# Where the modulation scale is applied: scaled features with one weight copy, against raw features with scaled and raw weight copies

## The chip, the cores and the metric

The kernel runs on one core of a Trainium2 chip. The metric is the device time of one execution in microseconds (us): three runs of the kernel before gave 404.8, 405.15 and 405.16 us, median 405.15. The profile is one further execution of the same program, with every instruction's start and length.

## The reference

The computation is one transformer-like block on x of 2,048 rows and 576 columns, in bfloat16, with six modulation vectors from a small product:

```
mod = silu(c) @ w_mod                      # six vectors of 576: sa, ca, ga, sb, cb, gb
h = layernorm(x) * (1 + ca) + sa
x = x + ga * attention(h, wqkv, w_phi, wo) # linear attention, 32 heads of 18
h = layernorm(x) * (1 + cb) + sb
x = x + gb * (relu(h @ w1) @ w2)           # 576 -> 4608 -> 576
```

In the attention, q and k of each head go through a small matrix w_phi (18 x 18); the features phi are softmax(p) and softmax(-p) side by side. kv is the sum over all rows of phi_k times v, z the sum of phi_k, and each row's output is (phi_q kv) / (phi_q z). All rows of K and V are needed before the first row of Q can be finished.

## The kernel before, in words

The 2,048 rows are 16 tiles of 128. The kernel has two stages. The first, up to about 102.6 us of the profiled execution, loads everything, does the modulation products, the projections K, V and Q of all tiles, kv, and the attention output, output projection and second norm of tiles 0 and 1. The second runs eight times over pairs of tiles: `l1` (first feed-forward product) and `l2` (second one, in a form with seven instead of eight quarter products), with the attention output of the next two tiles hung between. The change touches the first stage alone.

The norm is not applied to x. x is loaded transposed (xT: features on partitions, five chunks of 116), and a projection of a tile is ten matmuls of 288 columns (`proj`, L267): lhsT is xT's chunk, rhs the weight's. Mean and shift come in through four extra rows of the fifth chunk (`rows_copy`, L572, from per-row statistics; and their counterparts in the weights, made by `rows_mm`, `rows_h`, `rows_d`, L261 and L465 to L473, and by `quarters` for Q). The factor 1/std goes into the exponentials (`exps`, L273, ScalarE). w_phi is folded into the K and Q weights on the chip: `fold_all` (L426) for K, `fold_mm` (L250) for Q, products that end in PSUM and are copied to SBUF by ScalarE or VectorE (`f_raw` L437, `raw_copy` L513).

The factor (1 + ca), called `ca1`, is per feature, so it can be put on xT or on the weights. Before, it is put on xT: `x_scale` (L499) multiplies two tiles of xT in place, with five instructions on VectorE or ScalarE, or with one on GpSimd.

The order of the work in the first stage is a written list, `ORDER` (L43). Each word is a job (a function that issues instructions); each engine works through its own instructions in that order and waits on the others by semaphores. The names that matter:

- Z: matmuls on zeros without use (`spin`, L231). sc, sh: modulation products for ca and sa (`mods`, L241, 25 one-column matmuls each). ca: makes `ca1` and, from it, three columns of `m98` (L494); shc: the fourth column.
- FK: the fold of K. fra, frd, frr: copies of the folded K weight. xd, xa, xp: `x_scale` on VectorE, ScalarE, GpSimd.
- bn: row statistics (VectorE); sa, sp: what follows from them (ScalarE, GpSimd); T, Tc: transposed into the four rows.
- KR, VR, QR with Rh, Re, Rd: the weights' four rows. For Q they are four small DMAs (L485).
- K, V, Q: projections of a tile; Ka and Kb are its first four chunks and its last one. eK, eQ: exponentials. sK, rK, pA, pM: sums, reciprocals and scalings of phi_k (VectorE, ScalarE, GpSimd). vE: v out of PSUM, scaled. kv: accumulation, 9 matmuls, in PSUM banks 6 and 7.
- FQ with a chunk's number: the fold of Q, and FQra, FQrd its copies.
- qs, qp, qt: the same sums and scaling for phi_q, and the transposing DMA. sq, qi: phi_q stored to DRAM and read back. wo: output projection weight times ga (GpSimd), which needs ga_row, which comes by gaw and gar (two DMAs through DRAM).
- wl, w2a, w2b: loads of the feed-forward weights into regions R1 and R2 that the first stage's weights held before.
- kz, tp, nu, nO, ot, oc, W, xr, lb, lr, ap, ht, hd, ha: the way of tiles 0 and 1 from kv to the input of `l1`.

A number after a colon is one of four PSUM pairs of banks. A product into a pair waits until the pair's last content has been read. K's folded weight and Q's lie in `wk`, `wq` (region RH), V's is loaded straight to `wv`. SyncE issues the DMAs in the list's order; an issue that has to wait holds those behind it.

Of the kernel before, what the change touches and what calls it, by code (L numbers as in the profile page):

```python
# [7 lines left out]
P = 128  # L8
# [4 lines left out]
ACT = mybir.ActivationFunctionType  # L13
# [5 lines left out]
NC = 5  # L19
# [21 lines left out]


ORDER = """  # L43
Z11 sx sd rp sc bn1 Z2 bn0 FK ca sa0 sp0 fra0 frd4 sh fra1 frr fra2 xd0 T0:0 fra3 Z2 shc Tc0 Ka0:2 bn2 bn3
KR:1 xd2 sa2 Ka1:0 KRh0 sp2 KRh1 KRd0 Z2 KRd1 T2:1 Kb0 Tc2 Kb1 eKa0 FQ4:1 Z2 FQrd4 eKa1 bn4 FQ3:2 VR:1 sK0
FQra3 xp6 FQ1:0 VRh0 K2:2 FQra1 sK1 rK0 K3:0 VRh1 VRd0 rK1 VRd1 pA0 eK2 bn5 pM0 V0:1 eK3 sK2 m2:2 pA1 sa4 pM1
vE0 V1:0 m2c rK2 sK3 xa4 kv0 pA2 V3:2 sp4 vE1 pM2 bn7 kv1 rK3 T4:1 V2:0 bn9 Tc4 pA3 xa8 vE3 pM3 K4:1 vE2 K5:2
bn6 xp10 eK4 bn8 ga:0 kv2 eK5 sK4 kv3 V4:1 sa6 sK5 sa8 V5:2 sp6 gac sp8 rK4 bn12 rK5 T6:0 pA4 Tc6 wl0 pA5 vE4
xa12 K6:0 pM4 vE5 bn14 FQ0:1 K7:2 pM5 FQrd0 eK6 bn15 kv4 wl3 gb:1 eK7 xp14 kv5 sK6 V7:0 gbc sK7 rK6 T8:2 V6:1
Tc8 pA6 bn11 w2a1 rK7 K8:2 pM6 vE6 bn10 eK8 K9:1 pA7 w2a0 vE7 pM7 sa10 kv6 sK8 V8:2 eK9 sp10 bn13 kv7 rK8 gbw  # L50
T10:0 V9:1 wl1 Tc10 pA8 sK9 sa12 pM8 sa14 K10:0 vE8 rK9 K11:2 pA9 eK10 sp12 vE9 gbr pM9 wl4 kv8 eK11 V10:1
sK10 sp14 T12:0 sK11 w2a2 V11:2 rK10 Tc12 pA10 pM10 vE10 K13:0 rK11 w2b0 K12:1 eK13 pA11 vE11 pM11 kv9 eK12
T14:0 sK13 V13:2 Tc14 sK12 FQ2:1 rK13 K14:0 wl2 pA13 pM13 FQrd2 rK12 kv10 eK14 vE13 kv11 QR:1 K15:2 pA12 QRh
sK14 pM12 V14:0 gaw eK15 QRe QRd V15:1 rK14 sK15 pA14 gar V12:2 pM14 vE14 rK15 Q0:0 vE12 pA15 wo1 vE15 kv12
eQ0 Q1:2 pM15 Q2:1 qs0 eQ1 wo4 kv13 eQ2 kv14 qs1 kv15 qp0 Q3:0 sq2 tp0 Q4:2 qp1 eQ3 qt0 tp2 Q5:1 eQ4 sq3 wo3
tp1 qt1 Q6:0 eQ5 kz wo0 sq4 Q7:2 eQ6 wo2 qi2 nu0:3 Q8:1 w2b1 nO0 eQ7 nu1:0 eQ8 ot0:3 nO1 Q9:2 oc0 ot1:1 Q10:0
eQ9 sq6 sq7 W0:3 oc1 eQ10 sq9 W1:2 xr0 sq5 lb0 Q11:1 sq10 xr1 sq8 lr0 Q12:0 lb1 eQ11 Q13:3 ap0 qi3 lr1 eQ12
sq11 ht0:2 ap1 Q14:1 hd0 ha0 sq12 ht1:0 ha1 hd1 Q15:2 eQ14 qi4 eQ15 sq14 eQ13 sq15 sq13
"""

@with_exitstack
def tile_block(ctx, tc, a, out):
# [132 lines left out]
    def flat(v):  # L195
        return v.rearrange("p a b -> p (a b)")
# [2 lines left out]
    load(act, ident[:], "ident")  # L199
    load(sp, ccol[:], "cc")  # L200
    load(sp, flat(wsc), "wsc")
    load_x(0, 2)
    load(sp, flat(wkT), "wkT")
    load(sp, flat(wsh), "wsh")
    load_xT(0)
# [5 lines left out]
    load_x(4, 2)  # L211
    load_xT(2)
    load(sp, flat(wcb), "wcb")
    load(sp, flat(wsb), "wsb")
# [23 lines left out]
            dve.bn_stats(out=s[:, hf, :], in_=x_sb[:, t, hf * HD:(hf + 1) * HD])  # L238
        dve.bn_aggr(out=mv[:, n, t, :], in_=s)

    def mods(w, width, bank):  # L241

        o = PS[:, bank, :] if isinstance(bank, int) else bank[:, 0, :]
        for k, wm in enumerate(w):
            for ci in range(NC):
                for ck in range(NC):
                    pe.matmul(o[0:width, k * NC + ci:k * NC + ci + 1], lhsT=wm[0:R, ck, ci * width:(ci + 1) * width],  # L247
                              rhs=siluc[0:R, ck:ck + 1], start=(ck == 0), stop=(ck == NC - 1))
# [9 lines left out]
    def v2(ap):  # L258
        return ap.rearrange("p (b f) -> p b f", b=2)
# [174 lines left out]

    last = PS[0:R, 5, 0:NC * FW].rearrange("p (c f) -> p c f", f=FW)

    def f_raw(eng, ck):  # L437
        if eng is act:
            act.activation(out=wk[0:R, ck, 0:G5], in_=PS[0:R, ck, 0:G5], func=ACT.Copy)
        else:  # L440
            eng.tensor_copy(out=wk[0:R, ck, 0:G5], in_=PS[0:R, ck, 0:G5])

    w1a = carve(R1, 0, (4, DFF))
    w1b = R1[:, 4 * DFF:]
# [20 lines left out]
    def rows_h(pr, k):  # L465
        c = slice(k * HD, (k + 1) * HD)
        act.activation(out=tmpr[X0:NX, c], in_=pr[X0:NX, k, 0:HD], func=ACT.Copy)

    def rows_d(pr, dst, k):

        c = slice(k * HD, (k + 1) * HD)
        dve.scalar_tensor_tensor(out=dst[X0:NX, 4, c], in0=tmpr[X0:NX, c], scalar=mk[X0:NX, :],
                                 in1=pr[X0:NX, k, 0:HD], op0=ALU.mult, op1=ALU.add)  # L473

    def part(i):
        return ytb[:, D + i * QW:D + (i + 1) * QW]
# [19 lines left out]
        dve.tensor_scalar(out=m98[0:R, :, X0:X0 + 3], in0=ca1[0:R, :].unsqueeze(2).to_broadcast([R, NC, 3]), scalar1=-1.0,  # L496
                          scalar2=None, op0=ALU.mult)

    def x_scale(t, eng):  # L499

        xT, o, nt, j = XOFF[t]
        if eng is pool:
            v = xT[0:R, o:o + NC * nt * P].rearrange("p (c f) -> p c f", c=NC)[:, :, j * P:(j + 2) * P]
            pool.tensor_tensor(out=v, in0=v, in1=ca1[0:R, :].unsqueeze(2).to_broadcast([R, NC, 2 * P]), op=ALU.mult)
            return
        for ck in range(NC):
            v, f = xt(t, ck, 2), ca1[0:R, ck:ck + 1]
            if eng is act:
                act.activation(out=v, in_=v, func=ACT.Copy, scale=f)
            else:  # L510
                dve.tensor_scalar(out=v, in0=v, scalar1=f, scalar2=None, op0=ALU.mult)
# [77 lines left out]
    def k_minus(t):  # L589
# [376 lines left out]
```

The softmax here doesn't subtract the row's maximum and nothing guards it: scores larger than these inputs give would overflow.

## Time and profile before

| | us |
|---|---|
| median of three runs | 405.15 |
| the profiled execution's own time | 405.16 |
| its span, first to last instruction | 403.4 |
| TensorE busy in the span | 387.7 (96%) |
| VectorE, ScalarE, GpSimd busy | 238.0, 157.0, 147.3 |
| TensorE, VectorE, ScalarE, GpSimd busy in the first 100 us | 92.0, 70.3, 67.2, 55.5 |
| first matmul of `l1` (end of the first stage) | 102.57 |

The profile gives, for each engine, busy time and instructions; a row of tenths in 40 slices of the span; the chain of work that ended last; groups of instructions by line; and for any stretch the list of instructions in order of time. "PEclk" is the share of TensorE's full clock that was granted, in tenths. A product of ten matmuls of 288 columns goes by in 1.23 us at the full clock, one of nine for kv in 0.35 us.

### The profile page before, as it was taken

The numbers are of one execution on the slowest core, as the hardware profiler recorded it, in microseconds if no ns is written. First come the engines' busy times: TensorE is split into PE (matmuls) and PEld (weight loads), VectorE is DVE, ScalarE is ACT, GpSimd is POOL, SyncE is SP. The second block draws the span as 40 slices with busy tenths as digits, with TensorE's granted clock in tenths as the row PEclk, the third lists the DMA queues.
The fourth block names the chain that finished last, engine by engine and source line by source line (L and its number), as shares of the span: only waits on it lengthen the run. The fifth ranks groups of instructions, "written<-read, shape, count | busy, mean of one in ns | idle before, by whom it ended". The sixth has DMA issues, their size and how long they took to land.

```text
span 403.4 us, 8950 instructions
## 1 busy us (share of the span) xinstructions
PE 387.7 (96%) x3701; PEld 313.5 (78%) x3702; DVE 238.0 (59%) x463; ACT 157.0 (39%) x376; POOL 147.3 (37%) x202
## 2 busy tenths in 40 slices
PE   7999999878999998999999999999999999999996
PEld 4877788766887887778877887788788778878885
DVE  2689987845679955664655564547545646514222
ACT  2399887676741143103510530243034104402410
POOL 2157976760200341460066008301810470062045
PEclk9599999999999999999999999999999999999999
DMA  8999495187641155153006410610170061010000
GB/s 298 421 419 384 154 369 185 46 227 271 193 106 34 31 87 126 29 55 85 19 16 89 93 34 10 154 34 17 32 122 18 16 89 34 18 16 32 2 0 32
DMA packets 49517, 44.36 MB, mean 110 GB/s; under 512 B 39362, under 2 KB 42051, under 8 KB 48707
## 3 DMA queue, kind: packets, MB, share of 16 engines
q1 hardware_dynamic: 49186, 43.59, 38.6%
q8 instruction: 29, 0.48, 0.5%
q10 hardware_dynamic: 288, 0.19, 0.2%
q14 instruction: 14, 0.11, 0.1%
HBM read 27.97 MB, written 6.49 MB: 85 GB/s over the span
## 4 chain that ended last, share of the span: by engine, by line
PE 78%; DMA 7%; POOL 4%; DVE 4%; ACT 2%; issue 2%; SPq 1%; POOLq 0%; DVEq 0%; ACTq 0%
PE PS L671 31%; PE PS L731 23%; PE PS L270 9%; PE PS L678 5%; DVE h L857 3%; PE PS L804 3%; ACT RT L275 2%; DMA R<-in_wkT_dram 2%; PE PS L387 1%; DMA eqd<-RT 1%; PE PS L404 1%; POOL RH L743 1%; POOL RT L287 1%; DMA h<-xn 1%; PE PS L247 1%
## 5 line engine op out<-in xcount | busy, mean ns | idle before, releaser
L671 PE MATMUL PS<-h,R 128*128 128x256 bf16 x1152 | 134.3, 273 | 2.1 <-DVE h L857 2.1
L671 PEld LDWEIGHTS <-R 128*128 128x128 bf16 x1152 | 111.1, 98 | 18.8 <-issue 5.9
L731 PEld LDWEIGHTS <-RH 128*128 128x128 f16 x846 | 82.8, 98 | 20.8
L717 POOL TENSOR_TENSOR yt<-yt,gb_row 128x288 f32<-128x288 f32 x23 | 16.8, 729 | 187.3 <-DVE yt L716 187.3
L685 ACT ACTIVATE RH<-PS 128x256 f16<-128x256 f32 x72 | 27.5, 382 | 116.0 <-PE PS L678 101.0
L731 PE MATMUL PS<-R,RH 128*128 128x288 bf16 (+1 forms) x558 | 72.4, 286 | 0.0
L687 DVE SCALAR_TENSOR_TENSOR RH<-PS,RH 128x256 f16<-128x256 f32 x72 | 28.8, 413 | 62.7 <-ACT RH L685 62.7
L275 ACT ACTIVATE RT<-PS,rs 128x576 bf16<-128x576 f32 x64 | 42.7, 750 | 12.6 <-PE PS L270 7.0
L686 ACT ACTIVATE RH<-PS 128x512 f16<-128x512 f32 x72 | 42.9, 596 | 6.2 <-PE PS L671 5.2
L731 PE MATMUL PS<-RT,RH 128*128 128x288 f16 x288 | 37.9, 286 | 0.0
L735 ACT ACTIVATE RS<-PS 128x288 f32<-128x288 f32 x24 | 9.8, 410 | 69.2 <-PE PS L731 69.2
L270 PE MATMUL PS<-RH,RT 116*128 116x288 bf16 x240 | 31.8, 286 | 2.1 <-ACT RT L275 2.0
L270 PE MATMUL PS<-RH,R 116*128 116x288 bf16 x240 | 32.9, 291 | 0.5 <-ACT R L573 0.5
L743 POOL TENSOR_TENSOR RH<-RH,RT 128x2304 f16<-128x2304 f16 x7 | 31.8, 4548 | 0.0
L270 PEld LDWEIGHTS <-RT 116*128 116x128 bf16 x240 | 23.0, 98 | 8.1 <-issue 2.5
L270 PEld LDWEIGHTS <-R 116*128 116x128 bf16 x240 | 23.2, 99 | 7.0 <-issue 0.9
L238 DVE BATCH_NORM_STATS2 st<-x_sb 128x6 f32<-128x288 bf16 x64 | 25.9, 447 | 3.8 <-DMA x_sb<-in_xk_dram 3.2
L716 DVE TENSOR_TENSOR yt<-PS,RS 128x288 f32<-128x288 f32 x23 | 10.4, 451 | 29.7 <-POOL RH L743 24.0
L718 POOL TENSOR_TENSOR x_sb<-yt,x_sb 128x288 bf16<-128x288 f32 x31 | 22.4, 730 | 2.4 <-DVE yt L714 0.6
L280 DVE TENSOR_REDUCE Rk<-RT 128x64 f32<-128x1152 bf16 x16 | 21.1, 1343 | 2.3 <-ACT RT L275 2.0
L280 DVE TENSOR_REDUCE Rq<-RT 128x64 f32<-128x1152 bf16 x16 | 21.3, 1328 | 1.2 <-ACT RT L275 1.2
L409 DVE TENSOR_TENSOR x_sb<-x_sb,PS 128x576 bf16<-128x576 bf16 x16 | 12.0, 751 | 15.5 <-PE PS L804 8.1
(119 smaller groups left out, 439.3 us busy)
## 6 DMA issues: line engine op xcount, KB each, us to landing
R<-in_w1a_dram SPq DMA_DIRECT2D x4, 1152.0 KB, 14.3
eqd<-RT SPq DMA_DIRECT2D x14, 288.0 KB, 5.0
RT<-eqd SPq DMA_DIRECT2D x14, 288.0 KB, 3.0
R<-in_w2a_dram SPq DMA_DIRECT2D x3, 864.0 KB, 8.1
R<-in_w2b_dram SPq DMA_DIRECT2D x2, 1296.0 KB, 9.5
out_dram<-x_sb SPq DMA_DIRECT2D x15, 144.0 KB, 2.2
RT<-in_xT_dram SPq DMA_DIRECT2D x2, 640.0 KB
x_sb<-in_xk_dram SPq DMA_DIRECT2D x3, 288.0 KB
```

The lines of the kernel that those rows point to most:

```text
L238: dve.bn_stats(out=s[:, hf, :], in_=x_sb[:, t, hf * HD:(hf + 1) * HD])
L270: pe.matmul(pr[:, k, 0:HD], lhsT=xt(t, ck), rhs=w[0:R, ck, k * HD:(k + 1) * HD], start=(ck == 0), stop=(ck == NC - 1))
L275: act.activation(out=E.rearrange("p (b h s e) -> p b h s e", b=2, s=2, e=DH)[:, :, :, s, :], in_=pr[:, :, 0:HD].rearrange("p b (h e) -> p ...
L280: dve.tensor_reduce(out=Rr, in_=E.rearrange("p (c e) -> p c e", e=DH), axis=AXX, op=ALU.add)
L671: pe.matmul(PS[:, 2 * u + hf, n * 256:n * 256 + 256], lhsT=w1a[:, ci, jj * P:(jj + 1) * P], rhs=hb[:, ci, :], start=(n == 0 and ci == 0), ...
L678: pe.matmul(PS[:, 2 * u + hf, n * 256:n * 256 + 256], lhsT=w1b[b0:b0 + 64, j * P:(j + 1) * P], rhs=hb[b0:b0 + 64, 4, :], start=False, stop ...
L685: act.activation(out=A11[:, j, :], in_=lo[:, :, 0, :], func=ACT.Relu)
L686: act.activation(out=A2[:, j, :, :], in_=PS[:, 2 * u + 1, :].rearrange("p (n s f) -> p n s f", n=2, s=2), func=ACT.Relu)
L687: dve.scalar_tensor_tensor(out=U3[:, j, :], in0=lo[:, :, 1, :], scalar=0.0, in1=A11[:, j, :], op0=ALU.max, op1=ALU.subtract)
L718: pool.tensor_tensor(out=x_sb[:, t, c], in0=y, in1=x_sb[:, t, c], op=ALU.add)
L731: pe.matmul(PS[:, bank, 0:HD], lhsT=am[:, j, :], rhs=bm[:, j, :], start=first and j == 0, stop=(j % 9 == 8), skip_group_check=True)
L743: pool.tensor_tensor(out=A12, in0=A12, in1=U2, op=ALU.subtract)
```

## The change

`x_scale` is gone, and xT stays as it is loaded. The folded weights of K and Q are copied out of PSUM twice: once scaled by `ca1` into `wk` and `wq` (new jobs fs and fsd for K, fsr for its last 72 columns, FQs for Q) and once as they are into a new region `wfold` (fra, frd, frr, FQra, FQrd), which only the row products read. V's weight is loaded raw to a new region `wv_raw`, and five VectorE instructions (wsd) write it scaled to `wv`. The K and V row copies are one instruction over 576 columns where they were two over 288. `mods` gets a matmul on zeros ahead of each of its five groups in sc and sh (`idle=6`); of the separate Z matmuls 14 are left of 19. The first loads come in another order. And the list `ORDER` is a new one throughout the first stage, so that nearly every job changes its place: Q0 stands after K13 where it stood after V15, and qs0, qp0 and qt0 come forward with it; gbr, gaw and gar stand behind qt0; the five wo stand behind qp1; sq5 stands ahead of w2b1, and sq6 behind sq8. The second stage is the same.

```diff
+    wv_raw = carve(R1, 12760, (NC, D))
+    wfold = carve(R1, 15640, (NC, D))
...
-    load_x(0, 2)
     load(sp, flat(wkT), "wkT")
-    load(sp, flat(wsh), "wsh")
     load_xT(0)
+    load(sp, flat(wsh), "wsh")
+    load_x(0, 2)
+    load(sp, flat(wv_raw), "wv")
     load_x(2, 2)
     load_xT(1)
-    load(sp, flat(wv), "wv")
+    load_x(4, 2)
...
-    def mods(w, width, bank):
+    def mods(w, outs, width, bank, idle=None):
...
             for ci in range(NC):
+                if idle is not None:
+                    spin(1, idle)
...
+    def f_scaled_d(dst, ck):
+        dve.tensor_scalar(out=dst[0:R, ck, 0:G5], in0=PS[0:R, ck, 0:G5], scalar1=ca1[0:R, ck:ck + 1], scalar2=None, op0=ALU.mult)
+    def f_scaled(dst, ck):
+        act.activation(out=dst[0:R, ck, 0:G5], in_=PS[0:R, ck, 0:G5], func=ACT.Copy, scale=ca1[0:R, ck:ck + 1])
     def f_raw(eng, ck):
-            act.activation(out=wk[0:R, ck, 0:G5], in_=PS[0:R, ck, 0:G5], func=ACT.Copy)
+            act.activation(out=wfold[0:R, ck, 0:G5], in_=PS[0:R, ck, 0:G5], func=ACT.Copy)
...
-    def x_scale(t, eng):
...
+    def wv_scale(ck, eng):
+        o, i, f = wv[0:R, ck, :], wv_raw[0:R, ck, :], ca1[0:R, ck:ck + 1]
...
-    ROWS = {"K": wk, "V": wv, "Q": wq}
+    ROWS = {"K": wfold, "V": wv_raw, "Q": wfold}
+    ROWD = {"K": wk, "V": wv, "Q": wq}
...
+        "FQs": lambda c: act.activation(out=v2(wq[0:R, c, :]), in_=at["FQ", c][0:R, :, 0:HD], func=ACT.Copy, scale=ca1[0:R, c:c + 1]),
```

The head and the tail of the new list:

```
Z11 sx sd rp sc FK ca Z2 fs0 fsr frr fra2 sh frd4 fra0 fra1 bn1 fs3 bn0 fs1 Z1 fra3 shc sa0 wsd2 KR:0 fsd4 fs2
sp0 bn2 T0:2 VR:1 KRh bn3 Tc0 Ka0:2 KRd sa2 wsd1 sp2 VRh Kb0 wsd0 Ka1:0 wsd4 eKa0 VRd Kb1 wsd3 T2:1 eKa1 sK0
V0:2 Tc2 sK1 FQ3:0 rK0 K3:1 FQra3 pA0 FQs3 pM0 vE0 eK3 K2:0 bn4 bn5 rK1 kv0 eK2 FQ1:2 pA1 V1:1 sK3 pM1 FQra1
...
tp2 Q5:2 eQ4 sq3 tp1 wo3 nu0:3 eQ5 Q6:0 sq4 nO0 wo0 qi2 Q7:1 eQ6 wo1 sq5 ot0:2 w2b1 eQ7 nu1:3 Q8:0 nO1 oc0
Q9:1 eQ8 W0:3 eQ9 sq7 xr0 lb0 ot1:2 sq8 Q10:0 oc1 sq6 lr0 W1:1 ap0 eQ10 sq9 xr1 lb1 ht0:2 sq10 Q11:0 ha0 hd0
lr1 Q12:3 eQ11 ap1 Q13:2 qi3 eQ12 sq11 ht1:0 Q14:1 hd1 ha1 sq12 eQ13 Q15:3 qi4 eQ14 sq13 eQ15 sq14 sq15
```

More of the change, by code (lines that the diff above doesn't have):

```diff
@@ L43 @@
 ORDER = """
[L44 to L58, printed above, removed]
+Z11 sx sd rp sc FK ca Z2 fs0 fsr frr fra2 sh frd4 fra0 fra1 bn1 fs3 bn0 fs1 Z1 fra3 shc sa0 wsd2 KR:0 fsd4 fs2
@@ new lines @@
+sp0 bn2 T0:2 VR:1 KRh bn3 Tc0 Ka0:2 KRd sa2 wsd1 sp2 VRh Kb0 wsd0 Ka1:0 wsd4 eKa0 VRd Kb1 wsd3 T2:1 eKa1 sK0
+V0:2 Tc2 sK1 FQ3:0 rK0 K3:1 FQra3 pA0 FQs3 pM0 vE0 eK3 K2:0 bn4 bn5 rK1 kv0 eK2 FQ1:2 pA1 V1:1 sK3 pM1 FQra1
+m2:0 vE1 rK3 sa4 pA3 sK2 FQs1 kv1 sp4 V2:1 m2c pM3 bn7 rK2 T4:2 V3:0 bn6 Tc4 pA2 vE2 pM2 sa6 K4:2 vE3 K5:1
+bn10 eK4 sp6 bn9 T6:0 kv2 Tc6 kv3 eK5 sK4 ga:2 K7:0 gac sK5 rK4 K6:1 eK7 pA4 pM4 bn8 V4:2 eK6 sK7 gb:0 sa8
+V5:1 vE4 wl0 rK7 sp8 rK5 sK6 pA7 T8:2 gbc kv4 pA5 Tc8 FQ2:0 pM5 K8:2 vE5 rK6 FQrd2 K9:1 bn11 eK8 w2a2 pA6 pM6
@@ new lines @@
+bn14 kv5 sa10 V6:2 FQs2 sK8 eK9 sp10 wl1 V7:0 pM7 vE6 rK8 sK9 T10:1 V8:2 Tc10 pA8 vE7 pM8 K10:1 rK9 vE8 w2a0
+kv6 bn12 eK10 FQ0:0 pA9 FQ4:2 kv7 pM9 FQrd0 kv8 FQrd4 V9:1 FQs0 w2b0 bn13 FQs4 QR:0 vE9 K11:2 QRh sa12 QRe
+sK10 sp12 kv9 eK11 V10:1 bn15 QRd wl4 rK10 T12:0 V11:2 sK11 Tc12 pA10 sa14 pM10 K13:0 gbw vE10 rK11 wl2 Q0:1
+pA11 eK13 sp14 vE11 pM11 kv10 eQ0 T14:2 sK13 K12:0 w2a1 Tc14 qs0 kv11 rK13 K14:1 eK12 pA13 pM13 V13:2 eK14
+sK12 wl3 K15:0 qp0 vE13 rK12 sK14 V12:1 eK15 pA12 pM12 qt0 Q1:2 vE12 rK14 sK15 gbr V14:0 pA14 eQ1 gaw pM14
@@ L59 @@
+kv12 vE14 rK15 kv13 V15:1 qs1 pA15 gar pM15 kv14 Q2:2 vE15 qp1 kv15 eQ2 Q3:0 tp0 wo4 qt1 kz Q4:1 eQ3 wo2 sq2
+tp2 Q5:2 eQ4 sq3 tp1 wo3 nu0:3 eQ5 Q6:0 sq4 nO0 wo0 qi2 Q7:1 eQ6 wo1 sq5 ot0:2 w2b1 eQ7 nu1:3 Q8:0 nO1 oc0
+Q9:1 eQ8 W0:3 eQ9 sq7 xr0 lb0 ot1:2 sq8 Q10:0 oc1 sq6 lr0 W1:1 ap0 eQ10 sq9 xr1 lb1 ht0:2 sq10 Q11:0 ha0 hd0
+lr1 Q12:3 eQ11 ap1 Q13:2 qi3 eQ12 sq11 ht1:0 Q14:1 hd1 ha1 sq12 eQ13 Q15:3 qi4 eQ14 sq13 eQ15 sq14 sq15
 """
@@ L201, in tile_block @@
     load(sp, flat(wsc), "wsc")
+    load(sp, flat(wkT), "wkT")
+    load_xT(0)
+    load(sp, flat(wsh), "wsh")
     load_x(0, 2)
-    load(sp, flat(wkT), "wkT")
-    load(sp, flat(wsh), "wsh")
-    load_xT(0)
+    load(sp, flat(wv_raw), "wv")
     load_x(2, 2)
     load_xT(1)
-    load(sp, flat(wv), "wv")
+    load_x(4, 2)
     load(sp, epsr[:], "epsr")
     load(sp, flat(wqT), "wqT")
-    load_x(4, 2)
     load_xT(2)
@@ L435, in tile_block @@
     last = PS[0:R, 5, 0:NC * FW].rearrange("p (c f) -> p c f", f=FW)
+    def f_scaled_d(dst, ck):
+        dve.tensor_scalar(out=dst[0:R, ck, 0:G5], in0=PS[0:R, ck, 0:G5], scalar1=ca1[0:R, ck:ck + 1], scalar2=None, op0=ALU.mult)
+    def f_scaled(dst, ck):
+        act.activation(out=dst[0:R, ck, 0:G5], in_=PS[0:R, ck, 0:G5], func=ACT.Copy, scale=ca1[0:R, ck:ck + 1])
     def f_raw(eng, ck):
         if eng is act:
-            act.activation(out=wk[0:R, ck, 0:G5], in_=PS[0:R, ck, 0:G5], func=ACT.Copy)
+            act.activation(out=wfold[0:R, ck, 0:G5], in_=PS[0:R, ck, 0:G5], func=ACT.Copy)
         else:
-            eng.tensor_copy(out=wk[0:R, ck, 0:G5], in_=PS[0:R, ck, 0:G5])
+            eng.tensor_copy(out=wfold[0:R, ck, 0:G5], in_=PS[0:R, ck, 0:G5])
     w1a = carve(R1, 0, (4, DFF))
@@ L463, in t_part, with rows_h, rows_d @@
         eng.tensor_tensor(out=o[:, j, :], in0=p[:, j, :], in1=q[:, j, :], op=ALU.subtract)
[L465 to L473, printed above, removed]
+    def rows_h(pr):
+        act.activation(out=v2(tmpr[X0:NX, :]), in_=pr[X0:NX, :, 0:HD], func=ACT.Copy)
+    def rows_d(pr, dst):
+        dve.scalar_tensor_tensor(out=v2(dst[X0:NX, 4, :]), in0=v2(tmpr[X0:NX, :]), scalar=mk[X0:NX, :],
+                                 in1=pr[X0:NX, :, 0:HD], op0=ALU.mult, op1=ALU.add)
     def part(i):
@@ L497, in scale @@
                           scalar2=None, op0=ALU.mult)
-    def x_scale(t, eng):
[L501 to L511, printed above, removed]
     def raw_copy(eng, o, i):
@@ L517, in raw_copy @@
             eng.tensor_copy(out=o, in_=i)
+    def wv_scale(ck, eng):
+        o, i, f = wv[0:R, ck, :], wv_raw[0:R, ck, :], ca1[0:R, ck:ck + 1]
+        if eng is act:
+            act.activation(out=o, in_=i, func=ACT.Copy, scale=f)
+        else:
+            eng.tensor_scalar(out=o, in0=i, scalar1=f, scalar2=None, op0=ALU.mult)
     def turn(src, pr):
@@ L603, in tile_block @@
         "sd": silu, "ca": scale,
-        "sc": lambda: mods([wsc], R, 7),
-        "sh": lambda: mods([wsh], R, 7),
+        "sc": lambda: mods([wsc], None, R, 7, idle=6),
+        "sh": lambda: mods([wsh], None, R, 7, idle=6),
         "shc": lambda: dve.tensor_copy(m98[0:R, :, X0 + 3], PS[0:R, 7, 0:NC]),
         "FK": lambda: fold_all(wkT),
+        "fs": lambda c: f_scaled(wk, c), "fsd": lambda c: f_scaled_d(wk, c),
         "frd": lambda c: f_raw(dve, c), "fra": lambda c: f_raw(act, c),
-        "frr": lambda: dve.tensor_copy(out=wk[0:R, :, G5:D], in_=last),
+        "fsr": lambda: dve.tensor_tensor(out=wk[0:R, :, G5:D], in0=last,
+                                         in1=ca1[0:R, :].unsqueeze(2).to_broadcast([R, NC, FW]), op=ALU.mult),
+        "frr": lambda: dve.tensor_copy(out=wfold[0:R, :, G5:D], in_=last),
         "rp": lambda: pool.tensor_copy(rep[0:R], siluc[0:R, :].unsqueeze(2).to_broadcast([R, NC, 32])),
-        "xd": lambda t: x_scale(t, dve), "xp": lambda t: x_scale(t, pool), "xa": lambda t: x_scale(t, act),
+        "wsd": lambda c: wv_scale(c, dve), "wsa": lambda c: wv_scale(c, act), "wsp": lambda c: wv_scale(c, pool),
         "bn": lambda t: bn(0, t), "sa": stats_a, "sp": stats_p,
@@ L619, in tile_block @@
         "FQ": lambda c: fold_chunk(c, at["FQ", c]),
-        "FQrd": lambda c: raw_copy(dve, v2(wq[0:R, c, :]), at["FQ", c][0:R, :, 0:HD]),
-        "FQra": lambda c: raw_copy(act, v2(wq[0:R, c, :]), at["FQ", c][0:R, :, 0:HD]),
+        "FQs": lambda c: act.activation(out=v2(wq[0:R, c, :]), in_=at["FQ", c][0:R, :, 0:HD], func=ACT.Copy, scale=ca1[0:R, c:c + 1]),
+        "FQrd": lambda c: raw_copy(dve, v2(wfold[0:R, c, :]), at["FQ", c][0:R, :, 0:HD]),
+        "FQra": lambda c: raw_copy(act, v2(wfold[0:R, c, :]), at["FQ", c][0:R, :, 0:HD]),
         "Q": lambda t: proj(at["Q", t], t, wq), "eQ": lambda t: exps(t, at["Q", t], EQ[:, SLOT[t], :]),
         "sq": q_out, "qi": q_in, "qs": q_sm, "qp": q_pool, "qt": q_turn,
-        "m2": lambda: mods([wsb, wcb], P, at["m2", None]), "m2c": lambda: mod2_e(at["m2", None]),
+        "m2": lambda: mods([wsb, wcb], None, P, at["m2", None]), "m2c": lambda: mod2_e(at["m2", None]),
         "wo": lambda c: pool.tensor_tensor(out=wo_sb[:, c, :], in0=wo_sb[:, c, :], in1=ga_row[:], op=ALU.mult),
@@ L638, in tile_block @@
         JOBS[w + "R"] = lambda w=w: rows_mm(ROWS[w], at[w + "R", None])
-        for k in range(2):
-            JOBS[f"{w}Rh{k}"] = lambda w=w, k=k: rows_h(at[w + "R", None], k)
-            JOBS[f"{w}Rd{k}"] = lambda w=w, k=k: rows_d(at[w + "R", None], ROWS[w], k)
+        JOBS[w + "Rh"] = lambda w=w: rows_h(at[w + "R", None])
+        JOBS[w + "Rd"] = lambda w=w: rows_d(at[w + "R", None], ROWD[w])
     for i, w in enumerate("Q"):
@@ L645, in tile_block @@
         JOBS[w + "Re"] = lambda w=w, i=i: quarter_d(at[w + "R", None], i)
-        JOBS[w + "Rd"] = lambda w=w, i=i: quarter_rows(i, ROWS[w])
+        JOBS[w + "Rd"] = lambda w=w, i=i: quarter_rows(i, ROWD[w])
     for w, m, g in (("ga", wga, 0), ("gb", wgb, 1)):
```

## The prediction

> **What bounds the kernel now.** I read the page first. Its first line puts TensorE at 96% of the span; the row of tenths shows one hole in its clock, in the second slice (10.1 to 20.2 us):
>
> ```profile
> PE 387.7 (96%) x3701; PEld 313.5 (78%) x3702; DVE 238.0 (59%) x463; ACT 157.0 (39%) x376; POOL 147.3 (37%) x202
> PEclk9599999999999999999999999999999999999999
> ```
>
> Then the first stage in windows, with edges where the clock changes: it falls at 8.50 and is back at 18.75. That is 10.25 us, three times 3.41. Columns are length, then busy time of PE, weight loads, VectorE, ScalarE, GpSimd, then the granted clock.
>
> ```profile
> 5.09:8.50 3.41, 2.56 (x30) 1.55 (x28) 1.67 (x5) 0.00 (x0) 0.19 (x1) 1.00 1.03 417
> 8.50:11.92 3.42, 3.30 (x32) 3.31 (x33) 0.98 (x5) 2.55 (x7) 0.65 (x3) 0.50 1.03 413
> 11.92:15.33 3.41, 3.19 (x26) 2.66 (x27) 2.97 (x13) 0.38 (x1) 0.00 (x0) 0.50 1.00 416
> 15.33:18.75 3.42, 3.42 (x16) 2.63 (x15) 1.59 (x9) 1.00 (x4) 0.81 (x3) 0.50 1.04 421
> ```
>
> Next the timeline of TensorE in that stretch (start, length, what, what it waited for):
>
> ```profile
> 6.07 1.49 PE L247 MATMUL PS<-siluc,R 116*116 116x1 bf16 x25 [0.37 <-DMA R<-in_wsc_dram]
> 7.42 0.59 PE L233 MATMUL PS<-zero 128*128 128x512 bf16 x2
> 8.62 2.80 PE L432 MATMUL PS<-RS,R 126*116 126x126 bf16 x25 [0.60 <-DMA R<-in_wkT_dram]
> 11.22 2.64 PE L247 MATMUL PS<-siluc,R 116*116 116x1 bf16 x25
> 16.72 2.38 PE L264 MATMUL PS<-RH,RS 116*100 116x288 bf16 x10
> ```
>
> K's row product (L264) takes 2.38 us here and, later at full clock, V's takes 1.40. From 24 to 71 us TensorE runs on almost without a gap. Last, the timeline from there to the end of the stage, for its idle brackets:
>
> ```profile
> 77.09 0.52 PE L320 MATMUL PS<-RT 128*128 128x76 bf16 x9 [1.16 <-POOL RT L287]
> 84.69 0.55 PE L387 MATMUL PS<-kvz,RE 128*128 128x76 bf16 x10 [0.95 <-DMA RE<-RT]
> 88.44 1.39 PE L270 MATMUL PS<-RH,RT 116*128 116x288 bf16 x10 [0.66 <-ACT RT L275]
> 99.11 1.39 PE L270 MATMUL PS<-RH,RT 116*128 116x288 bf16 x10 [1.33 <-ACT RT L275]
> ```
>
> So the stage is bound by TensorE at half clock, then by TensorE at full clock with VectorE nearly full beside it (9.80 of 10 us in both slices from 30 to 50), then by waits: GpSimd behind ga_row (wo1 waited 2.36 us for it at 74.14, and pM15, qp0, qp1 stood behind it), the transposing DMA behind those, and at 97.68 ScalarE's eQ11, 2.56 us behind the store sq5. What follows 102.57 is the same code in both kernels and starts from l1's first matmul: a shift of that start is carried to the end.
>
> [...] The window that lost the clock streamed columns for some 1.03 us (0.60 of the first Z, 0.43 of the two at 7.42), 30%; the windows 83.60 to 87.02 and 97.26 to 100.67, with 47% and about 44% by the same count, kept it. [...] For VectorE's wsd, 116x576 from SBUF, L418's 414 ns for the same shape is the nearest row[...].
>
> **The change, start of the stage.** Laid out by hand: each engine's jobs in the new order, each as soon as its inputs and its engine are ready, with the trace's durations (back to back where they overlap).
> - Loads move at 0.43 MB/us. wsc lands at 6.07 as before; wkT now follows it, 0.74 MB, so 7.8 (before 8.5). xT0 8.6, wsh 10.3, x tiles 0-1 at 11.0 (before 6.8), wv 12.7, x 2-3 13.4.
> - sc: 25 matmuls at 0.06 and five Z at 0.213: 5.9 to 8.45. In the window to 8.50 the columns streamed are then 0.60 + 5 x 0.213 = 1.67 us, 49%, above the 44% that kept the clock: I take it that the clock stays full. FK from 8.45, 25 matmuls at 0.06 (L255's pace at full clock): 10.0. Z2 10.4, sh 2.5 us: 12.9. The next two windows come to about 65% and 57%.
> - ScalarE: fs0 9.05, then six more at 0.51 to 0.58: fra3 ends 12.8. The doubled copies cost 2.1 us on ScalarE (fs) and 1.2 on VectorE (fsr, fsd4), all ahead of the first product. VectorE from 10.2: fsr 0.5, frr 0.5, frd4 0.65, bn1 and bn0 1.96, shc: 14.0.
> - KR waits for shc, and T0, VR and Ka0 are queued behind it; fs2 is behind sa0, which waits for bn0. KR 14.0 to 15.3, T0, VR to 16.75, Ka0 to 17.7, Kb0 (after KRd, 17.8) 18.1. The first exponential starts at 18.3 where it started at 21.07.
> - Then sK0, V0 (after VRd and wsd3) to 21.1, and with a wait of 0.7 for FQs3 on the way, V1 ends at 26.85. By then K0 to K3, V0, V1, KR, VR, two FQ and kv0 are done. Before had K0 to K3, V0, KR, VR and three FQ by 28.2: after is 1.35 us earlier and V1 (1.23) and kv0 (0.8) less one FQ (0.31) further. **3.1 us ahead.**
>
> **The middle.** Removed: 10 instructions of L511 (2.1 us back to back) from VectorE, 15 of L509 (6.3) from ScalarE, 3 of L504 (2.32 each, 7.0) from GpSimd. Added there: wsd 5 x 0.33 = 1.7 on VectorE, FQs 5 x 0.65 = 3.2 on ScalarE. Merging K's and V's row copies saves some 0.3 us on each. Since TensorE and VectorE set the pace here, GpSimd's 7 us are worth nothing by themselves. From 26.85 TensorE has 28 products of K, V and Q (34.3), three FQ (0.95), kv1 to kv13 (4.7), six T (0.8), m2 1.27, ga and gb 0.86, QR 0.43: 43.3, to 70.15. VectorE, laid out beside it, is full but for 1.5 us in all and holds TensorE up by 0.5. V15 ends at 70.7, with Q0, Q1, kv12 and kv13 done too; before, the last V product ended at 71.05 without them. That is 0.35 + 2 x 1.23 + 2 x 0.35 = **3.5 us ahead**, 0.4 more than at the start. On SyncE: QRd is issued from 53.6 and lands at 58.2, Q0 needs it at 59.0; FQ0 waits for wl1's transfer (its region overlaps the Q weight), issued at 41.3, 1.18 MB, landed by 46, needed at 49.6; qt0 stands ahead of gbr, gaw, gar and holds them until qp0 ends at 66.1, so ga_row lands at about 73.5, and wo4 is due at 74.5. All three are covered, by 0.8, 3.6 and 1.0 us; lost cover costs the excess, on TensorE.
>
> **The tail.** From 70.7: 14 Q (17.2), kv14 and 15 (0.7), nu 0.74, ot and ht 1.1, W 2.46: 22.2 us of products. Before, from 71.05: 25.3 of products, and 102.57 was reached, so 6.2 us of waits (4.9 of them in brackets). pM15 and qp1 no longer stand behind wo; qt0 and qt1 are done before nu needs them; sq5 is issued ahead of the 1.3 MB of w2b1. In the layout pM15 ends at 72.25, qp1 at 74.5, the five wo (1.27 each) at 80.9, nO0 at 80.6, W0 runs at 83.9 and W1 at 86.6, ht1 at 92.6. The waits come to 2.5 us (kv15 for pM15, ot0 for nO0 behind tp1 and tp2, ht1 for eQ11): l1 at 95.4, 7.2 us earlier. But a layout by hand has no late semaphores or queueing DMAs, so I allow the tail twice that, 5.0: l1 at 97.9, **4.7 us earlier**. Against the profiled execution's own 405.16 (median 405.15, the same): 400.5.
>
> Bounds of what the trace doesn't show: the clock kept (0) or lost for one window at 15.33 (1.7 us of the 3.41) or from 8.50 on (below); tail waits from 2.5 to 6.2.
>
> **The rivals.**
> - Slower: the clock falls at 8.50 all the same[...]. Then FK takes 2.80 (to 11.25), Z2 0.85, sh 2.44 + 5 x 0.43 = 4.6 (to 16.7), KR 2.38, T0, VR 2.38 (to 22.0); [...] eKa0 at 23.5, 5.2 us later than laid out. With the tail's waits as before (6.2, not 5.0): 400.5 + 5.2 + 1.2 = 406.9. It decides once more than 4.7 us go. For it: FK at 70 to 80% of the window 8.50 to 11.92 didn't raise the clock before. Against: the 44% that kept it.
> - No change: the stage is VectorE's. To the last vE it has 61 us of work from 10.2 on; in the layout it idles 1.5 us; before, it idled some 5 us between 55 and 75. If it does so again 3.5 us of the gain go, and 404.1 is left; with a late ga_row beside it, 405.
> - A partial gain: the clock lost only at 15.33, KR being late by 1 us: 402.2 to 403.
>
> **How the numbers follow.** The gain as worked out, 398.0 (the layout's 7.2) to 402.0: 0.48. Partial, to 404.3: 0.12. Within 0.2% of 405.15, 404.3 to 406.0, which is about what a measurement of this kernel can tell from no change: 0.10. Slower, by the clock, 406 to 408: 0.30. The likeliest gives 400.5, with its own range 398.0 to 402.0. The range over the cases is 398.0 to 407.0: 0.05 lie below, 0.12 above.
>
> **What would show it.** Right: a granted clock of 1.00 from 5 to 20 us, eKa0 at 18.3, V15's end near 71 with Q0 and Q1 done, no wait of GpSimd for ga_row, l1's first matmul at 96 to 99. Wrong: PEclk of 5 in the second slice, and FK at 2.8 us; VectorE with brackets of 0.5 us and more from 30 to 60; TensorE waiting for FQs copies (a pair of banks now freed by two copies instead of one); or a second stage that waits for weights loaded later.

## The result, and the profile after

The changed kernel takes 396.14 us (median of four runs, 395.76 to 396.28) against 404.98 (404.75 to 405.16): a ratio of 0.9781, 95% interval 0.9764 to 0.9798. It was forecast faster, at 400.5, and the range ended at 398.0: the way was right and the size was not, 8.8 us where 4.7 were expected. Measured again later, the changed kernel came out at 395.94 and 395.76, while single executions of the kernel before spread from 400.45 to 406.54. The stretch at half clock that its profile shows, its clock hole of 10.25 us, is of changing length from one execution to the next (6.82 us in a profile below), so a comparison with it has to say which hole it means.

The page of the changed kernel, the same two lines:

```profile
PE 383.6 (97%) x3706; PEld 310.7 (79%) x3707; DVE 237.8 (60%) x458; ACT 156.6 (40%) x368; POOL 139.3 (35%) x199
PEclk9999999999999999999999999999999999999999
```

The 5 in the second slice of the clock is gone. GpSimd has lost 8.0 us of busy time, 7.0 of them the three products of `x_scale`; ScalarE and VectorE have lost next to nothing, as new copies took the place of the old products. The windows (length, busy time of PE, weight loads, VectorE, ScalarE, GpSimd, granted clock, share and rate of DMA) at the same edges:

```profile
5.09:8.50 3.41, 3.41 (x31) 2.29 (x29) 0.00 (x0) 0.00 (x0) 0.19 (x1) 1.00 1.01 405
8.50:11.92 3.42, 3.36 (x51) 2.92 (x51) 1.99 (x6) 2.81 (x6) 0.00 (x0) 1.00 1.00 410
11.92:15.33 3.41, 2.66 (x28) 2.21 (x28) 3.34 (x11) 2.09 (x6) 0.65 (x3) 1.00 1.06 420
15.33:18.75 3.42, 3.42 (x31) 2.93 (x30) 3.18 (x10) 2.70 (x7) 0.61 (x3) 1.00 1.01 419
```

TensorE's timeline from the fold on, and then the end of the stage (start, length, what, in brackets the idle time ahead and what ended it):

```profile
8.65 1.58 PE L436 MATMUL PS<-RS,R 126*116 126x126 bf16 x25
13.92 1.40 PE L268 MATMUL PS<-R,RS 116*100 116x288 bf16 x10 [0.75 <-DVE RS L608]
...
82.38 1.26 PE L408 MATMUL PS<-wo_sb,oT 128*128 128x288 bf16 x9 [0.31 <-POOL wo_sb L631]
86.61 0.45 PE L529 MATMUL PS<-ident,xn 128*128 128x128 bf16 x5 [0.24 <-DVE xn L422]
87.41 3.83 PE L274 MATMUL PS<-RH,RT 116*128 116x288 bf16 x30 [0.34 <-ACT RT L279]
93.81 3.22 PE L676 MATMUL PS<-h,R 128*128 128x256 bf16 x28
```

The fold runs in 1.58 us instead of 2.80, K's row product (L268) in 1.40 instead of 2.38. At the end three brackets of 0.2 to 0.35 us stand where before there were six of 0.29 to 1.33, and the first matmul of `l1` is at 93.81, 8.76 us earlier than at 102.57. From there to the end of the span it is 300.6 us, against 300.8 before: the whole gain was made in the first stage.

### The profile page after: what moved, and what is told of

It reads as the page before. It is cut to its first block, busy times and chain, and to the rows that moved or that the text cites. A ratio compares the mean times of both kernels' runs of the same rounds, so it can differ in the third digit from the quotient of the medians.

```text
span 394.4 us, 8939 instructions
## 1 busy us (share of the span) xinstructions
PE 383.6 (97%) x3706; PEld 310.7 (79%) x3707; DVE 237.8 (60%) x458; ACT 156.6 (40%) x368; POOL 139.3 (35%) x199
## 4 chain that ended last, share of the span: by engine, by line
PE 79%; DVE 6%; POOL 5%; DMA 4%; ACT 3%; issue 2%; SPq 0%; POOLq 0%; DVEq 0%; ACTq 0%
PE PS L676 32%; PE PS L736 24%; PE PS L274 8%; PE PS L683 5%; DVE h L862 3%; PE PS L809 3%; POOL wo_sb L631 2%; PE PS L408 2%; PE PS L235 2%; ACT RT L279 1%; PE PS L391 1%; POOL RH L748 1%; DMA gatd<-gt 1%; DMA h<-xn 1%; DVE st L240 1%
## 5 line engine op out<-in xcount | busy, mean ns | idle before, releaser
L274 PE MATMUL PS<-RH,R 116*128 116x288 bf16 x240 | 31.8, 286 | 0.5 <-ACT RH L625 0.5
```

The lines of the kernel that those rows point to most:

```text
L274: pe.matmul(pr[:, k, 0:HD], lhsT=xt(t, ck), rhs=w[0:R, ck, k * HD:(k + 1) * HD], start=(ck == 0), stop=(ck == NC - 1))
```

## The experiments

All times are medians. "The tail" is the first stage from the last V product on. Theory C says that the gain came from the clock and from the order of the tail, theory S that it came from the place of the scale, that is from the work taken off the engines by dropping `x_scale`.

### The spins alone

```diff
+    def mods(w, width, bank, idle=None):
...
+                if idle is not None:
+                    spin(1, idle)
...
+        "sc": lambda: mods([wsc], R, 7, idle=6),
+        "sh": lambda: mods([wsh], R, 7, idle=6),
```

> The kernel before with one thing added: a matmul on zeros ahead of each of the five groups in the two modulation products sc and sh (ten in all). Theory C (clock and order): the window 5.09 to 8.50 then streams about 49% instead of 30%, the clock stays at 1.00 from 5 to 20 us, the fold FK takes 1.5 us instead of 2.8, the first exponential starts near 18 instead of 21.07, and the time falls by about 3 us, to 401.5 to 402.5. Rival S (place of the scale): the gain of the change came from the work that x_scale took off GpSimd, ScalarE and VectorE; the spins alone give under 1 us, 404 to 405. If the clock falls all the same, the ten spins cost 1 to 2 us: 406.

Measured: 400.91 against 403.39, ratio 0.9942 (0.9921 to 0.9964), about 2.3 us, a little faster than expected. What these 2.3 us are is told by the mean granted clock that was taken with each execution. The 10.25 us at half clock of the profile before, in 403.4, make a mean of 0.987. The later executions of the kernel before, 39 in all, and those with the spins, by this clock; in brackets, as an estimate, the time at half clock that it stands for, twice the share that is missing of some 403 us:

| mean granted clock | kernel before: executions, us | with the spins: executions, us |
|---|---|---|
| 0.985 to 0.987 (10 to 12 us) | 13, 403.94 to 405.74, median 404.81 | none |
| 0.989 to 0.992 (6 to 9 us) | 10, 403.05 to 403.97, median 403.43 | none |
| 0.996 (3 us) | none | 2, 401.80 and 402.81 |
| 0.998 to 1.00 (under 2 us) | 11, 400.45 to 401.71, median 401.07 | 18, 399.28 to 401.46 |

Five more of the kernel before have 0.998 to 1.00 and took 404.51 to 406.54; no trace explains these. For the others the spins are worth what a kept clock is worth: about 4 us against an execution with 10 to 12 us at half clock, next to nothing against one with under 2. The 2.3 us lie between because the kernel before had both kinds.

The profiled execution is the slowest of the 20, 402.81 us, so its end is not the usual one. The clock stays at 1.00 over its whole start (5.09 to 18.75) and the fold takes 1.56 us; the products K2, K3, V0 begin at 20.53 instead of 24.36, 3.8 us earlier. But in this execution `l1` starts only 1.4 us earlier, at 101.17. ScalarE's timeline and TensorE's show where the rest went; the first line is the same place in the kernel before, the second the kernel with the spins:

```profile
97.68 1.38 ACT L275 ACTIVATE RT<-PS,rs 128x576 bf16<-128x576 f32 x2 [2.56 <-DMA eqd<-RT]
95.17 1.38 ACT L277 ACTIVATE RT<-PS,rs 128x576 bf16<-128x576 f32 x2 [3.47 <-DMA eqd<-RT]
```

```profile
73.66 0.52 PE L322 MATMUL PS<-RT 128*128 128x76 bf16 x9 [1.54 <-POOL RT L289]
96.60 1.39 PE L272 MATMUL PS<-RH,RT 116*128 116x288 bf16 x10 [2.24 <-ACT RT L277]
```

eQ11 waits for the store sq5 3.47 us (2.56 before), TensorE behind it 2.24 (1.33 before), and pM15 1.54 (1.16 before). The last microsecond is in the clock, window by window (granted clock third from the end):

```profile
98.00:99.00 1.00, 0.72 (x6) 0.64 (x6) 0.39 (x2) 1.00 (x4) 0.00 (x0) 0.54 0.68 262
99.00:100.00 1.00, 1.00 (x6) 0.62 (x5) 0.92 (x4) 1.00 (x3) 0.00 (x0) 0.50 0.81 308
100.00:101.00 1.00, 1.00 (x6) 0.63 (x5) 1.00 (x1) 0.98 (x2) 0.00 (x0) 0.50 0.47 71
101.00:102.00 1.00, 1.00 (x9) 0.78 (x8) 0.54 (x2) 0.59 (x1) 0.27 (x2) 0.75 0.76 279
```

The longer wait left ten matmuls in the 3.4 us before 98.1, by the count of columns that the prediction uses an estimated 35% of that time (2,880 columns, at 0.213 us for 512), and behind it the clock was at half here too, for 3.4 us by these four lines; the last Q product took 2.60 us, where the one ahead of it took 1.39, and the transposes ahead of it 0.69 instead of 0.45. So in this execution the head start was lost in a queue, and the clock fell behind it; that the one brought the other about is not shown. This is not what the median execution does: by its time, 400.91, some 4 us less than an execution of the kernel before with 10 to 12 us at half clock, the head start came through.

### The order of the tail alone

```diff
-eK10 sp12 vE9 gbr pM9
+eK10 sp12 vE9 gbr gaw gar pM9
-... V14:0 gaw eK15 ... pA14 gar V12:2 ... pA15 wo1 vE15 ... eQ1 wo4 kv13
+... V14:0 eK15 ... pA14 V12:2 ... pA15 vE15 ... eQ1 kv13
-qp1 eQ3 qt0 ... kz wo0 sq4 Q7:2 ... xr0 sq5 lb0
+qp1 wo1 wo4 eQ3 qt0 ... kz wo0 sq4 sq5 Q7:2 ... xr0 lb0
```

> The kernel before with only its order changed near the end of the first stage: gaw and gar directly behind gbr, so that ga_row is there early; wo1 and wo4 behind qp1 instead of ahead of pM15 and qp0; sq5 ahead of w2b1 instead of behind sq9. Theory C: the waits of 1.16 (for pM15), 0.95 and 0.49 (for the transposing DMA) and 1.33 us (for eQ11 behind sq5) go, l1 starts 2.5 to 4 us earlier, 401 to 402.5; the clock stays at 0.5 from 8.5 to 18.75. Rival S: ScalarE and the banks bind the tail anyway, under 1 us: 404 to 405.

Measured: 398.29 against 403.39, ratio 0.9873 (0.9804 to 0.9941). That is 5.1 us and more than was expected. In its profile one bracket of 0.28 us is left in the whole tail, and `l1` starts at 94.88:

```profile
82.97 1.39 PE L270 MATMUL PS<-RH,RT 116*128 116x288 bf16 x10 [0.28 <-ACT RT L275]
94.88 3.22 PE L671 MATMUL PS<-h,R 128*128 128x256 bf16 x28
```

The profiled execution had a shorter clock hole than the kernel before's, from 8.90 to 15.72, 6.82 us instead of 10.25, so some 2 us of the 7.7 by which its `l1` is earlier are not the tail's. Its four executions took 395.72 us (clock 0.998), 397.63 (0.990), 398.95 and 399.23 (0.987): against the medians of the kernel before at the same clock 5.3 to 5.8 us less, whatever the hole.

### Both, and twice

> The kernel before with both edits, the spins in the modulation products and the order near the end of the stage; x is still scaled in place and each weight copied once. Theory C: the two add up, 398 to 399.5, so most of the change's 8.8 us is had without moving the scale. Rival S: 403 to 405.

Measured: 394.65 against 403.39, ratio 0.979 (0.9745 to 0.9835): 8.7 us, and over 3 us faster than expected. Run again beside the changed kernel on one chip:

> The kernel before with the spins in the modulation products and the new order of its tail, once more, beside the changed kernel on the same chip. It differs from the changed kernel in the place of the scale (on xT, with one copy of each weight) and in the order of the middle. Theory C: the place of the scale is worth nothing either way, both at 394.3 to 396.3 and within 0.3% of each other. Rival S': the doubled copies cost the changed kernel 1 to 2 us, so that this one is ahead by that: 394.3 to 395 against 396.

> The changed kernel, unaltered, for that comparison. Every theory: 395.4 to 396.4.

Measured: 395.0 (394.9 to 395.13) for this one and 395.76 (395.52 to 397.03) for the changed kernel, five runs each. Both reach `l1` at about the same time, 93.13 and 92.94. So scaled features with one copy of each weight are, with spins and tail mended, as fast as raw features with two copies, and in these runs 0.8 us ahead; of that the profiles show nothing in the first stage (from `l1` on 300.2 us pass in the one and 300.8 in the other, in code that is the same). This is the fastest version that was run. Theory S falls: everything that the change gained is to be had without moving the scale. What the changed kernel itself owes to its spins is measured below; what it owes to its tail is read from its profile, since no run put the old order back into it. Nor was the order of its middle tested apart from the place of the scale.

### The two halves of the tail

Both on the kernel with the spins, which alone took 400.91. First the ga_row part (gaw, gar, wo1, wo4), then the sq5 part of the diff above.

> The kernel before with the spins in the modulation products, and of the new order of the tail only the first part: gaw and gar directly behind gbr, and wo1 and wo4 behind qp1. sq5 stays behind sq9. The kernel with the spins alone took 400.9 us and showed waits of 1.54 us for pM15, 0.95 and 0.49 for the transposing DMA, 0.66, and 2.24 for eQ11. If GpSimd's queue behind ga_row is the larger part: those four waits go and eQ11's stays or grows by up to 1 us, 397 to 398.5. If sq5 is the larger part: the products run earlier into the wait for sq5, 399 to 400.5.

> The kernel before with the spins in the modulation products, and of the new order of the tail only the second part: sq5 directly behind sq4, ahead of w2b1. wo1 and wo4, gaw and gar stay where they were. If GpSimd's queue behind ga_row is the larger part: only eQ11's wait of 2.24 us goes, 398.5 to 399.5. If sq5 is the larger part: 396 to 397.5.

Measured: 396.91 with the ga_row part, 398.91 with the sq5 part, 394.65 and 395.0 with both: 4.0, 2.0 and about 6 us. The halves add. (The 400.91 and 394.65 are from another chip than the rest; the kernel with both parts differs by 0.35 us between the two.) TensorE's brackets of the first:

```profile
80.94 1.39 PE L272 MATMUL PS<-RH,RT 116*128 116x288 bf16 x10 [0.31 <-ACT RT L277]
91.25 1.39 PE L272 MATMUL PS<-RH,RT 116*128 116x288 bf16 x10 [0.98 <-ACT RT L277]
92.93 0.44 PE L530 MATMUL PS<-ident,xn 128*128 128x128 bf16 x5 [0.29 <-ACT RT L277]
```

and of the second:

```profile
73.21 0.52 PE L322 MATMUL PS<-RT 128*128 128x76 bf16 x9 [1.04 <-POOL RT L289]
80.79 0.55 PE L389 MATMUL PS<-kvz,RE 128*128 128x76 bf16 x10 [0.93 <-DMA RE<-RT]
83.04 0.55 PE L389 MATMUL PS<-kvz,RE 128*128 128x76 bf16 x10 [0.48 <-DMA RE<-RT]
84.53 1.39 PE L272 MATMUL PS<-RH,RT 116*128 116x288 bf16 x10 [0.66 <-ACT RT L277]
```

Each edit takes away the brackets that it was aimed at. The others stay or get shorter: eQ11's is 0.98 us with the ga_row part alone, where it was expected to keep its 2.24 or grow, and pM15's is 1.04 instead of 1.54 with the sq5 part alone; the 2.24 and the 1.54 are those of the slowest execution. The larger part is GpSimd's queue: one small store and one broadcast through DRAM, issued late (at 64.23 and 71.02 in the profile before, the second behind QRd's four from 68.28 on), held up a multiplication by ga that nobody needed yet, and behind it the work that everybody needed.

### The changed kernel without its spins, and once more as it is

```diff
-        "sc": lambda: mods([wsc], None, R, 7, idle=6),
-        "sh": lambda: mods([wsh], None, R, 7, idle=6),
+        "sc": lambda: mods([wsc], None, R, 7),
+        "sh": lambda: mods([wsh], None, R, 7),
```

> The changed kernel without the ten spins in sc and sh, nothing else. Theory C: the window to 8.50 falls to some 18% (only the first Z), the clock goes to 0.50 there and stays for three or four windows, FK takes 2.8 us, and the time rises by 3 to 5 us, 399 to 401. Rival S: FK and the row products keep the clock or its loss is covered by other engines, 396 to 397.

> The changed kernel once more, unaltered, beside the three below on the same chip, since the kernel before took 400.5 to 405.1 us in the last call and 404.8 to 405.2 in the first. Every theory: 395.5 to 396.7, its clock being 1.00 throughout.

Measured: 398.54 without, just below what was expected, and 395.94 as it is; the spins are worth 2.6 us here. The clock falls near 7.7, comes back near 11.1, falls again near 14.5 and is back near 17.95: the stretch ahead of the second fall, with Z, sh and a wait of 1.23 us for shc, is thin as well, with 2.18 us of TensorE in 3.41. Windows (as above):

```profile
7.85:11.07 3.22, 3.00 (x28) 2.73 (x28) 0.82 (x2) 2.59 (x5) 0.00 (x0) 0.50 1.02 413
11.07:14.48 3.41, 2.18 (x31) 1.90 (x31) 3.34 (x11) 1.91 (x7) 0.47 (x3) 0.99 1.03 414
14.77:17.95 3.18, 3.18 (x16) 2.81 (x15) 2.92 (x9) 1.75 (x6) 0.62 (x3) 0.50 1.02 425
```

### The price of scaling, and the price of copying twice

Scaling left out, on the kernel before with spins and tail (all words xd, xa, xp taken out of the list; the projections then lack the factor 1 + ca):

> The kernel before with the spins and the new order of its tail, and with x_scale left out: xT is never multiplied by 1 + ca, so the projections lack that factor; nothing takes its place. It measures the whole price of scaling the features: 2.1 us of VectorE, 6.3 of ScalarE, 7.0 of GpSimd. Theory C (clock and order): these engines have room there, at most 0.6 us, from the two blocks of 1.05 us on VectorE ahead of the first exponentials: 394.0 to 394.7. Rival S (place of the scale): 390 to 392.

Measured: 395.74, no faster than the 394.65 and 395.0 with it. In its profile the whole start is late, from the first products of `siluc` on (6.39 instead of 5.51): those of K0 begin at 13.49 instead of 12.66, and `l1` at 93.64 instead of 93.08, so it is even with it or 0.3 us ahead. Both expectations were off. From the start of K2 to the end of the last V product 46.7 us pass without the scaling (21.12 to 67.82) and 46.7 with it (20.59 to 67.30, in the second run of spins and tail). 15 us of work on three engines cost nothing that can be measured, in this order of the tail; on the kernel before as it stands the scaling was not left out.

Raw copies left out, on the changed kernel:

```diff
-    ROWS = {"K": wfold, "V": wv_raw, "Q": wfold}
+    ROWS = {"K": wk, "V": wv_raw, "Q": wq}
...
-fs1 Z1 fra3 shc sa0 wsd2 KR:0 fsd4 fs2
+fs1 fs2 Z1 shc sa0 fsd4 wsd2 KR:0
```

> The changed kernel without the raw copies of the folded K and Q weights (fra, frd, frr, FQra, FQrd); the row products of K and Q read the scaled copies instead, so the mean's and the shift's terms carry the factor 1 + ca once too often. fs2 and fsd4 stand ahead of KR, which now needs them. It measures the price of copying twice: 2.1 us on ScalarE and 1.2 on VectorE ahead of the first product. Theory C: VectorE's chain to the first exponential gets up to 1.2 us shorter, part of it is taken back in the tail: 394.9 to 395.8. Rival S: the second copies are hidden, 396.0 to 396.4.

Measured: 394.74 (394.60 to 395.29) against 395.94 (395.37 to 396.81), 1.2 us: just below what was expected. K's row product starts at 12.98 instead of 13.45, though the first product of `siluc` came 0.2 us later (6.27 instead of 6.07): on VectorE frr and frd4 are gone from ahead of shc. `l1` starts at 92.61 instead of 92.98. So the profiles give the second copies a price of 0.4 to 0.6 us in the first stage. The rest of the 1.2 is in no profile, the profiled executions (395.29 and 395.37) being nearly equal. That price is what the place of the scale costs the changed kernel.

### One step that failed

The kernel before with spins and tail, without its three later pairs of zero matmuls:

```diff
-fra3 Z2 shc ... KRd0 Z2 KRd1 ... FQ4:1 Z2 FQrd4
+fra3 shc ... KRd0 KRd1 ... FQ4:1 FQrd4
```

> The kernel before with the spins in the modulation products and the new order of its tail (394.65 in the last call), and without the three later pairs of matmuls on zeros (ahead of shc, between KRd0 and KRd1, behind FQ4). With the clock kept at 1.00 the stage is now bound by TensorE, so the 6 x 0.213 = 1.3 us they take on it should come off, if the products behind them don't wait for something else just then: 393.3 to 394.3, ahead of the changed kernel by 2 to 3 us. Against it: the copies of K's fold and its rows (VectorE) are what the products there wait for, then 394.5 as before. If the clock falls in one of the windows there, 396 or more.

Measured: 396.06, so nothing was gained. `l1` starts at 93.08, where it did with them; to the hundredth that is chance, as this execution's first product of `siluc` came at 6.30 and that one's at 5.51. The two with a like start, 6.30 here and 6.16 with the spins alone, show it better: K0 begins at 12.61 instead of 12.91, but K2 at 20.55 and 20.53. What came off ahead of K0 went into waits behind it, where the zeros had run in time that TensorE would have waited in:

```profile
16.50 0.27 PE L572 MATMUL PS<-ident,sc 128*100 128x128 bf16 x2 [0.54 <-DVE RH L474]
18.69 0.47 PE L257 MATMUL PS<-RS,R 126*116 126x126 bf16 x6 [0.91 <-ACT RT L277]
```

Between K0 and K2 the pace is set by VectorE's rows and ScalarE's first exponential, which end these two brackets, not by TensorE. Why the median is 1 us above that of the kernel with the zeros is known in part. Two of the four executions, 396.49 and 396.77, have a mean clock of 0.994 and 0.995, which stands for an estimated 4 to 5 us at half clock; the other two, with 0.998 and 1.00, took 395.60 and 395.64. None of the nine with the zeros has less than 0.998. So the zeros seem to have had a use after all, though no profile shows where the clock fell. What is left, 0.6 us and more, stays open: the profiled spans differ by 0.7 us (393.8 and 393.1) with `l1` starting at the same time, so it lies in the second stage, which is the same in both.

## Why the prediction was right in its way and wrong in its size

**The clock: right.** It stayed full over the whole start, 1.00 in all four windows from 5.09 to 18.75. That 49% of columns streamed would be enough was the author's estimate, made from the 44% of another stretch; at what share the clock falls no run shows, so the 49% itself is not tested. That it is the spins that keep it is shown from both sides: put into the kernel before they fill the hole (1.00 from 8.50 to 18.75 where it was 0.50), taken from the changed kernel they open it (0.50 from 7.7 to 11.1 and from 14.5 to 17.95). The fold was expected to end at 10.0 and ended at 10.2.

**The start: right.** The first exponential was expected at 18.3 and came at 18.20; V1 was expected to end at 26.85 and was through at 26.8. The waits of KR for shc and of K2 for FQs3 are there (0.75 and 0.49 us). That it fits to a tenth is luck in part: the first product of `siluc` came at 6.39 in this profile, at 5.52 and 6.07 in two later ones of the same kernel, and `l1` began at 93.81 here and at 92.94 and 92.98 there.

**The middle: right.** V15 was expected to end at 70.7 and ended at 70.24, with Q0, Q1, kv12 and kv13 done. VectorE did not become the bound, nor did the two copies hold up a pair of banks more than once. The 43.3 us of products took 43.4, so the 0.5 that VectorE was to cost did not come.

**The tail: this step failed.** It found 2.5 us of waits in the layout and then said: "But a layout by hand has no late semaphores or queueing DMAs, so I allow the tail twice that, 5.0". From 70.24 to 93.81 are 23.6 us, 22.2 of them products: the waits were 1.4. That one term is 3.6 us too large, and with the 0.5 of the middle makes up the whole miss (97.9 against 93.81 for `l1`). The allowance has no working of its own: it is the layout's 2.5 doubled, which brings it near the 6.2 of the kernel before. But those 6.2 were no general friction of the tail: with the spins in, the experiments take 4.0 us away with two words moved ahead and two moved back, and 2.0 with one, and 0.3 us of brackets are left. Waits that are traced to named causes should have gone with the causes.

The layout itself was 1.1 us too slow there. It put nO0's end at 80.6; VectorE was through with it at 78.56, tp1 and tp2 having ended at 77.4. In the other direction, ga_row was expected at 73.5, ahead of wo4; GpSimd waited for it until 74.88, because gaw, issued at 67.45, took 4.29 us to land. First the wait in the kernel before, then in the changed one:

```profile
74.14 1.27 POOL L625 TENSOR_TENSOR wo_sb<-wo_sb,ga_row 128x576 bf16<-128x576 bf16 x1 [2.36 <-DMA ga_row<-gatd]
74.88 7.45 POOL L631 TENSOR_TENSOR wo_sb<-wo_sb,ga_row 128x576 bf16<-128x576 bf16 x5 [2.24 <-DMA ga_row<-gatd]
```

W0 paid 0.31 us for that, the first of the three brackets shown. So "no wait of GpSimd for ga_row", named as a sign of being right, did not come true, and it hardly mattered: in the old order the wait and the two wo products behind it were worth 4.0 us (2.72 us of wait, on the kernel with the spins), here 2.24 us of wait cost 0.3. What counts is what is queued behind it.

**The shares: partly wrong.** The sum gave 3.1 of its 4.7 us to the start, 0.4 to the middle and 1.2 to the tail. By its own reckoning the profile gives 4.0 to start and middle (0.81 us earlier at V15's end, and the same four products further) and 4.8 to the tail (6.2 of waits less 1.4). The kernel before says much the same at equal clock: about 4 us for the clock if 10 to 12 us run at half, 5.3 to 5.8 for the tail, some 10 for both (394.65 and 395.0 against 404.81). The tail is the larger part. **The slower rival** (the clock falls all the same, and is back at a time that was the author's estimate) was wrong: with the spins in, the clock was 1.00 from 5 to 20 us. **The rival of no change** (VectorE) was wrong (its 404.1 is 404.0 by its own sum, 400.5 and 3.5). That GpSimd's 7 us would be worth nothing by themselves was right, as `b_st_noscale`, the run without scaling, shows for ScalarE's and VectorE's part as well.

## What to carry to other kernels

Here the layout by hand from the trace's durations was 1.1 us too slow in the tail and the allowance on top of it 2.5: an allowance for unknown friction near the old kernel's waits counts again the very waits that the new order removes. Read a change by its parts in the order, not by its name: here the named part, where a factor is applied, was worth nothing or a little less, and two side effects, zero matmuls among thin products and a list in which late data hold up nobody, were worth the whole gain. And look at more than one execution before a profile is taken for the median: the profiled one of the kernel with the spins was the slowest of 20. In a queue that is worked off in its order, as GpSimd's is here (in the kernel before wo1 waited 2.36 us for ga_row, pM15 came behind it, and TensorE waited 1.16 for that), put work whose input comes late, and whose result is needed late, behind everything else.

## What was not expected of the hardware

The clock hole is not in step with the program: it opened at 8.50 in one profile of the old start and at 8.90 in another, that of the new tail alone, though the first product of `siluc` came at 6.07 in the first and at 5.73 in the second, and it lasted 10.25 us in the first and 6.82 in the second. Most of the spread of the kernel before comes from this, 400.45 to 406.54 us over all later executions against 395.37 to 397.03 for the changed kernel, whose three profiled executions have a mean clock of 0.998 to 1.00: in 34 of the 39 the time goes with the mean granted clock, and in 11 of these it is 0.998 or more. So the 8.8 us of the result hold against executions with the long hole, such as the profiled one; against those that keep the clock, at some 401.07, the change gains 4.9. That this is near the 4.7 of the prediction is chance, as it was reckoned from the profile with the hole.

And the clock fell far into a kernel, too: in the profiled execution with the spins alone, a wait of 2.24 us in a stretch of few products came just ahead of a fall to 0.50 at 98.1. One other of the 20 has as low a mean clock, 0.996.
